# Attention and token mixer on one core: the seventh pair turned within the sixth step, the first batch's third products split over two steps

## The chip, the core and the metric

The kernel runs on one core of a Trainium2 chip. The core has a matrix engine (PE), which multiplies and transposes and writes only to PSUM, a memory of eight banks; a vector engine (DVE) and a scalar engine (ACT), which read PSUM and move results to the main on-chip memory; GpSimd (POOL), which here scales v and issues the loads; and SyncE (SP), which here issues most stores. Each engine takes its instructions in the order written and waits on semaphores for the others. The metric is the device time in microseconds (us) of one launch; lower is better. "Before" was run six times: median 99.96 us, 99.41 to 102.1.

## The reference

There are 4 batches, 8 heads, 768 tokens and 64 numbers a head. Attention without softmax and with a decay goes by blocks, with a running state of 64x64 for each head; its output is the x of a token mixer.

```python
for b in range(nb):
    intra = np.einsum('bhic,bhjc->bhij', qb, kb) * Dmask[None]
    intra = np.einsum('bhij,bhjd->bhid', intra, vb)
    inter = np.einsum('bhid,bhde->bhie', qb * lam_pow[None], kv_state)
    out[:, :, sl] = intra + inter
    kv_state = lam_block[None, :, None, None] * kv_state + np.einsum('bhsd,bhse->bhde', kb_dec, vb)
...
wq = x @ w_q
wk = x @ w_k
W_tok = scale * np.einsum('bsd,btd->bst', wq, wk)
mixed = np.einsum('bst,btd->bsd', W_tok, x)
return (np.maximum(mixed, 0.0) @ w_out).astype(np.float32)
```

`Dmask` is lower triangular with powers of lam, and `scale` is 1/8.

## The kernel before

**Pairs and steps.** Two heads of one batch are a pair; there are 16, four to a batch. The main loop (L563) makes one step a pair, n = 0 to 15. In this document "step n" and "pair n" use that count from 0, so the sixth step is step 5 and the seventh pair is pair 6. Tokens go in chunks of 128, six to a head. The decays are powers of lam put into q (`dq`) and v (`DvI`), so that the mask `maskc` is only ones and zeros.

**What a pair needs.** Three loads from POOL, `fq`, `fk` and `fv` (`load_q` L81, `load_kv` L86), 192 KB each as they land. `turn_q` (L231) transposes q with 12 PE instructions into the bank `trq`, and DVE makes qT from it, times `dq`. `turn_k` (L253) does the same into `trk`, and ACT copies it out as kT. `scale_v` (L208) makes vn, mostly on POOL. `scores` (L307) makes four banks `sc` from kT and qT, `masks` (L327) has DVE turn each into `pr`. `states` (L269) multiplies k by vn into `dps`, which holds the sums of all earlier chunks, and `sums` (L287) copies them to gs. `inter` (L334) multiplies qT by gs into two banks `oa`, `values` (L351) adds pr times vn to them, and ACT copies them to xnat, the pair's piece of x. `flip` (L375) transposes that to xT, through the bank `xp`.

**Step n** does the scores and masks of pair n, `inter` and `values` of pair n-1, the flip of pair n-2, the states and sums of pair n, and the turns of pair n+1, whose q and k must have landed by then. PE's order in it is scores, inter, values, flip, turn_q, turn_k, states.

**The mixer of a batch** runs during later steps. `mix_wk` (L396) and `mix_wq` (L416) make wkn and wqT from xT. `mix_py` (L439) multiplies wkn by xnat; ACT copies the result three times into Y. `mix_pm` (L463) makes the mixed values, 128x384 at a time, each in a bank `pm`; ACT and DVE in turn take relu and 1/8 into rmT. These are the "third products" of the change's name: eight for a batch, two for each block of 128 columns `dd`. `mix_po` (L508) multiplies rmT by the output weights `wo`, four PE instructions for 128 tokens, and ACT copies the result to osb. For batch 0 the flip of pair 3 and `mix_wk` are at the end of step 4; `mix_wq`, `mix_py`, all eight `pm` and then both turns of pair 6 are in step 5; output products of batch 0 are in steps 6 to 10 (`outs` before the turns, `late_outs` after the states).

**Order and buffers.** The order on each engine is the order of the program text; waits are put in from the data used. PSUM banks are handed out by a list: `pst` (L58) takes the bank that was free longest, `done` (L64) puts one back, and the next user of a bank waits until the engine that last read it has done so. Four banks `pm` and four `sc` are all eight.

**Loads.** All of q, k, v (but the first k), the mixer's `wqk` and `wo` are issued by POOL in program order. The start takes pairs 0 to 4; L547 to L553 issue q5, k5, `wqk`, v5 and `wo`; the dictionary `pool` (L556) gives POOL's work of steps 0 to 4 ("s4" is the scaling of v of pair 4), and later steps use `load_more` (L220). Each POOL load waits until the eighth load issued before it has landed. Stores of batch 0 wait in the list `stores` until the small transfer `late` (L579) of step 9, which waits for a late load of v.

Of the kernel before, what the change touches and what calls it, by code (L numbers as in the profile page):

```python
# [28 lines left out]
def kernel(  # L29
# [11 lines left out]
    nc = tc.nc  # L41
# [16 lines left out]
    def pst(shape, dt, name):  # L58
        i = free.pop(0)
        t = ps.tile(shape, dt, tag=f"p{i}", name=name)  # L60
        held[id(t)] = (t, i)
        return t

    def done(t):  # L64
        free.append(held.pop(id(t))[1])

    pairs = [(b, kk) for b in range(B) for kk in range(NP)]
    N = len(pairs)
# [4 lines left out]
    def q_rows(n):  # L73
        b, kk = pairs[n]
        return q[b, 2 * kk : 2 * kk + 2].rearrange("h (a p r) d -> p h a (r d)", p=128, r=2)

    def kv_rows(n, src):
        b, kk = pairs[n]
        return src[b, 2 * kk : 2 * kk + 2].rearrange("h (c p) d -> p h c d", p=128)

    def load_q(n):  # L81
        t = stage.tile([128, 2, 3, 2 * D], BF16, tag="fq", name="fq")
        nc.gpsimd.dma_start(out=t, in_=q_rows(n))  # L83
        staged[n, "q"] = t

    def load_kv(n, nm):  # L86
        t = stage.tile([128, 2, NCH, D], BF16, tag="f" + nm, name="f" + nm)
        nc.gpsimd.dma_start(out=t, in_=kv_rows(n, dict(k=k, v=v)[nm]))  # L88
        staged[n, nm] = t
# [137 lines left out]
    def turn(n):  # L227
        turn_q(n)
        turn_k(n)

    def turn_q(n):  # L231
        b, kk = pairs[n]
        fq = staged.pop((n, "q"))
        trq = pst([128, NCH, 2, 64], BF16, "trq")
        for a in range(3):
            for r in range(2):
                for hl in range(2):
                    nc.tensor.transpose(  # L238
                        trq[hl * 64 : hl * 64 + 64, 2 * a : 2 * a + 2, r, :],
                        fq[:, hl, a, r * D : (r + 1) * D],  # L240
                        ident,
                    )
        qT = tsb.tile([128, S], BF16, tag="qT", name="qT")
        nc.vector.tensor_tensor(  # L244
            out=qT,
            in0=trq.rearrange("d c r p -> d (c r p)"),
            in1=Dq[kk],
            op=ALU.mult,
        )
        done(trq)  # L250
        L[n]["qT"] = qT
# [75 lines left out]
    def masks(n, which):  # L327
        for a, hl in which:
            t = prb.tile([128, 3, CH], BF16, tag="pr", name="pr")
            nc.vector.tensor_tensor(out=t, in0=L[n]["sc"][a, hl], in1=maskc, op=ALU.mult)  # L330
            done(L[n]["sc"][a, hl])
            L[n]["pr"][a, hl] = t
# [83 lines left out]
    def mix_wq(b, kts=range(NP)):  # L416
        if 0 in kts:
            M[b]["wq"] = pst([128, HALF], F32, "wq")
        wq = M[b]["wq"]
        for kt in kts:  # L420
            for n in range(2):
                nc.tensor.matmul(  # L422
                    wq[n * 64 : n * 64 + 64, :],
                    wqk[:, 0, kt, :],
                    xT[b][:, kt, n * HALF : (n + 1) * HALF],
                    start=(kt == 0),
                    stop=(kt == NP - 1),
                    skip_group_check=True,
                )
        if NP - 1 in kts:  # L430
            wqT = hyp.tile([128, HALF], BF16, tag="wqT", name="wqT")
            nc.scalar.copy(
                out=wqT.rearrange("j (c p r) -> j c r p", c=3, r=2),
                in_=wq.rearrange("j (c r p) -> j c r p", c=3, r=2),
            )
            done(wq)
            M[b]["wqT"] = wqT
# [25 lines left out]
    def mix_pm(b, which, wide=True, engs=None):  # L463

        if isinstance(which[0], int):
            which = [(dd, n) for dd in which for n in range(2)]
        pms = [pst([128, HALF], F32, "pm") for _ in which]
        for m in range(1 if wide else 2):
            for (dd, n), pm in zip(which, pms):
                r = slice(n * 64, n * 64 + 64)  # L470
                c = (dd % 2) * CH
                if wide:
                    o, w = slice(0, 128), slice(c, c + CH)
                else:
                    o, w = slice(m * 64, m * 64 + 64), slice(c + m * 64, c + m * 64 + 64)
                nc.tensor.matmul(  # L476
                    pm[o, :],
                    M[b]["Y"][r, int(dd // 2 != n), w],
                    M[b]["wqT"][r, :],
                    start=True,  # L480
                    stop=True,
                    skip_group_check=True,
                )
        for i, ((dd, n), pm) in enumerate(zip(which, pms)):
            to = M[b]["rmT"][:, dd, n * HALF : (n + 1) * HALF]
            if engs and engs[i] is nc.vector:
                nc.vector.tensor_scalar(  # L487
                    out=to,
                    in0=pm,
                    scalar1=1.0 / 8.0,  # L490
                    scalar2=0.0,
                    op0=ALU.mult,
                    op1=ALU.max,
                )
            else:
                nc.scalar.activation(out=to, in_=pm, func=ACT.Relu, scale=1.0 / 8.0)
            done(pm)
# [10 lines left out]
    def mix_po(b, t, last=False):  # L508
# [39 lines left out]
    load_kv(5, "k")  # L548
    load_wqk()
    load_kv(5, "v")  # L550
    nc.gpsimd.dma_start(
        out=wo, in_=moe_w_out.rearrange("(kt p) (a j) -> p a kt j", p=128, j=CH)
    )  # L553


    pool = {  # L556
        0: ["q6", "s4", "k6", "v6"],
        1: ["q7", "s5", "k7", "v7"],
        2: ["q8", "k8", "s6", "v8"],
        3: ["q9", "s7", "k9", "v9"],  # L560
# [2 lines left out]
    for n in range(N):  # L563
        b, kk = pairs[n]
        for what in pool.get(n, []):
            if what[0] == "s":
                scale_v(int(what[1:]), nc.gpsimd)
            elif what[0] == "q":
                load_q(int(what[1:]))
            else:  # L570
                load_kv(int(what[1:]), what[0])
        if 11 <= n + 5 < N:
            load_more(n + 5)
        if n + 5 >= N and n + 3 < N:
            scale_v(n + 3, nc.gpsimd)
        if n == 9:

            late = consts.tile([1, D], BF16, name="late")
            nc.sync.dma_start(out=late, in_=staged[14, "v"][0:1, 0, 0, :])  # L579
            store()  # L580
        p = b - 1
        outs = {
            6: [(0, 0)],
            9: [(0, 4)],
            12: [(1, 0)],
            13: [(1, 2)],
            14: [(1, 3)],
            15: [(1, 5)],
        }.get(n, [])

        late_outs = {
            6: [(0, 1)],
            7: [(0, 2)],
            8: [(0, 3)],
            10: [(0, 5)],
            12: [(1, 1)],
            14: [(1, 4)],
        }.get(n, [])

        def back():  # L600

            if kk == 1 and n > 8:
                flip(n - 2, nc.scalar)
            if n >= 1:
                values(n - 1)
            if n >= 2 and not (kk == 1 and n > 8) and n != 5:
                flip(n - 2, nc.scalar if n < 5 else None)
            for i, t in outs:
                mix_po(i, t)
            if kk == 1 and n > 8:  # L610
                mix_wk(p)


        if n > 9 and n % 4 in (3, 0):
            mix_pm(
                (n - 5) // 4,
                [0, 1] if n % 4 == 3 else [2, 3],
                engs=(nc.scalar, nc.vector) * 2,
            )
        scores(n)  # L620
        if n >= 1:
            inter(n - 1)
        masks(n, ((0, 0), (0, 1)))
        back()

        if 1 <= n < 3:
            make_dq(n + 1)
        if n in (2, 3):
            scale_v(n, nc.vector)
        masks(n, ((1, 0),))  # L630
        if n < N - 1 and n != 5:
            turn_q(n + 1)
        masks(n, ((1, 1),))
        if n < N - 1 and n != 5:
            turn_k(n + 1)
        if n == 5:

            mix_wq(p)
            mix_py(p)
        states(n)  # L640
        if n == 4:
            flip(n - 1)
        for i, t in late_outs:
            mix_po(i, t)
        sums(n)
        if n == 0:
            scale_v(1, nc.vector)
        if n == 4:
            mix_wk(p, (0, 1, 2))
            mix_wk(p, (3,))  # L650
        if n == 5:
            for dds in ([0, 1], [2, 3]):
                mix_pm(0, dds, engs=(nc.scalar, nc.vector) * 2)
            turn(n + 1)
        if kk == 1 and n > 8:
            mix_wq(p)
            mix_py(p)
# [53 lines left out]
```

## Time and profile before

| | us |
|---|---|
| median of six runs | 99.96 |
| the profiled execution: its own time | 99.95 |
| its span, first to last instruction on the core | 98.1 |
| PE busy in the span | 85.6 |
| DVE busy | 70.9 |
| ACT busy | 62.4 |
| POOL busy | 66.8 |
| first scores of step 5 (PE) | 28.2 |
| first scores of step 6 | 34.8 |
| first scores of step 7 | 39.2 |
| first scores of step 8 | 42.8 |
| first scores of step 9 | 46.3 |
| first scores of step 10 | 51.7 |

The span's 98.1 us lie within the execution's 99.95; 1.85 us are around it. Times of single events below are counted from the span's start. Busy time is how long an engine had an instruction in work; matmuls overlap, and their ends are modelled, so a full PE isn't at its peak. A step with an output product or more of the mixer's work is longer. The loads' transfer engines are nine tenths busy or more from 2.5 to about 69 us. The clock of PE is granted in full but for one stretch at half, from 20.35 to 23.76 us.

### The profile page before, as it was taken

To read this page: it belongs to the slowest core of one execution; us is meant where nothing else is said; L and a number is where in the kernel's file an instruction comes from. 1 tells how busy PE (TensorE), PEld (TensorE's weight loads), DVE (VectorE), ACT (ScalarE), POOL (GpSimd) and SP (SyncE) were. 2 spreads that over 40 slices of the span, in tenths; PEclk is the share of its full clock that TensorE was granted. 3 is DMA by queue.
4 is the path that set the end of the run, shared out by engine and by line. 5 is a ranking of instruction groups with operands and counts; after the bars stand their busy time and mean duration, and the time that the engine had idled before them with its cause. 6 is when DMAs were issued, how large, how long until landed. Compare 5 with 4: busy or idle time off the path is not lost.

```text
span 98.1 us, 3522 instructions
## 1 busy us (share of the span) xinstructions
PE 85.6 (87%) x1507; PEld 58.0 (59%) x1507; DVE 70.9 (72%) x156; ACT 62.4 (64%) x118; POOL 66.8 (68%) x69
## 2 busy tenths in 40 slices
PE   4998677399998789999999996999999999999940
PEld 1335566387986465966788474668865466433420
DVE  6647989785976977899489999973989981273520
ACT  5085487866749945665769764667977746677230
POOL 5999999999999399999999999999060000000000
PEclk9999999966999999999999999999999999999999
DMA  0999999999999999999999999999999424325583
GB/s 7 215 148 159 166 161 162 166 164 160 168 187 157 166 168 156 145 147 134 135 153 160 133 156 132 139 141 123 272 404 395 178 107 176 145 107 213 215 313 115
DMA packets 68976, 16.79 MB, mean 171 GB/s; under 512 B 65762, under 2 KB 66018, under 8 KB 68962
## 3 DMA queue, kind: packets, MB, share of 16 engines
q0 software_dynamic: 63776, 9.90, 138.7%
q1 hardware_dynamic: 5042, 6.56, 18.4%
q8 instruction: 11, 0.18, 0.7%
q10 hardware_dynamic: 144, 0.13, 0.4%
q14 instruction: 3, 0.02, 0.1%
HBM read 20.19 MB, written 6.29 MB: 270 GB/s over the span
## 4 chain that ended last, share of the span: by engine, by line
PE 58%; DVE 15%; ACT 11%; DMA 6%; POOL 3%; issue 3%; POOLq 0%; ACTq 0%
PE po L515 19%; PE oa L359 6%; DMA fk<-in_k_dram 6%; DVE pr L330 5%; PE xp L379 5%; PE sc L317 5%; PE trq L238 5%; DVE rmT L487 4%; PE trk L258 4%; PE wq L422 3%; PE py L443 3%; PE dps L277 3%; PE wk L402 2%; ACT kT L262 2%; PE oa L341 2%
## 5 line engine op out<-in xcount | busy, mean ns | idle before, releaser
L330 DVE TENSOR_TENSOR pr<-sc,maskc 128x384 bf16<-128x384 f32 x64 | 33.3, 548 | 3.0 <-PE sc L317 2.7
L515 PE MATMUL po<-wo,rmT 128*128 128x512 bf16 (+1 forms) x100 | 23.9, 372 | 0.0
L212 POOL TENSOR_TENSOR vn<-fv,DvI 128x768 bf16<-128x768 bf16 x12 | 18.0, 1502 | 4.7 <-PE xp L379 2.8
L371 ACT CAST xnat<-oa 128x384 bf16<-128x384 f32 x31 | 13.4, 483 | 8.6 <-PE oa L359 8.5
L527 ACT COPY osb<-po 128x512 f32<-128x512 f32 (+1 forms) x22 | 12.6, 579 | 9.7 <-PE po L515 9.7
L262 ACT COPY kT<-trk 128x768 bf16<-128x768 bf16 x16 | 12.8, 801 | 7.2 <-PE trk L258 7.2
L88 POOL DMA_DIRECT2D fv<-in_v_dram x16 | 16.9, 1054 | 0.0
L88 POOL DMA_DIRECT2D fk<-in_k_dram x15 | 16.0, 1063 | 0.0
L83 POOL DMA_DIRECT2D fq<-in_q_dram x16 | 14.0, 876 | 0.8 <-POOLq L695 0.8
L515 PEld LDWEIGHTS <-rmT 128*128 128x128 bf16 x100 | 8.5, 98 | 8.5 <-issue 0.8
L317 PE MATMUL sc<-qT,kT 64*128 64x128 bf16 x192 | 8.9, 217 | 3.6 <-ACT kT L262 1.3
L244 DVE TENSOR_TENSOR qT<-trq,dq 128x768 bf16<-128x768 bf16 x16 | 8.8, 552 | 4.1 <-PE trq L238 2.9
L317 PEld LDWEIGHTS <-kT 64*128 64x128 bf16 x192 | 5.9, 94 | 8.1 <-ACT kT L262 5.6
L258 PE MATMUL trk<-ident,fk 128*64 128x128 bf16 x180 | 8.0, 226 | 2.4 <-DMA fk<-in_k_dram 2.4
L238 PE MATMUL trq<-ident,fq 128*64 128x128 bf16 x192 | 8.7, 229 | 0.0
L359 PE MATMUL oa<-vn,pr 128*128 128x64 bf16 x192 | 8.6, 196 | 0.0
L487 DVE TENSOR_SCALAR rmT<-pm 128x384 bf16<-128x384 f32 x16 | 8.0, 548 | 0.6 <-PE pm L476 0.6
L379 PE MATMUL xp<-ident,xnat 128*128 128x128 bf16 x96 | 8.3, 225 | 0.2
L277 PE MATMUL dps<-vn,fk 128*64 128x128 bf16 (+4 forms) x150 | 8.0, 239 | 0.0
L258 PEld LDWEIGHTS <-fk 128*64 128x64 bf16 x180 | 6.1, 114 | 3.1 <-DMA fk<-in_k_dram 3.1
L238 PEld LDWEIGHTS <-fq 128*64 128x64 bf16 x192 | 6.1, 113 | 3.1 <-issue 2.2
L359 PEld LDWEIGHTS <-pr 128*128 128x128 bf16 x192 | 6.8, 99 | 0.7
(62 smaller groups left out, 113.7 us busy)
## 6 DMA issues: line engine op xcount, KB each, us to landing
out_dram<-osb SPq DMA_DIRECT2D x23, 256.0 KB, 3.1
fq<-in_q_dram POOLq DMA_DIRECT2D x16, 192.0 KB, 5.7
fv<-in_v_dram POOLq DMA_DIRECT2D x16, 192.0 KB, 5.6
fk<-in_k_dram POOLq DMA_DIRECT2D x15, 192.0 KB, 6.2
wo<-in_moe_w_out_dram POOLq DMA_DIRECT2D x1, 512.0 KB, 9.4
k<-in_k_dram SPq DMA_DIRECT2D x1, 384.0 KB, 3.8
out_dram<-osb ACTq DMA_DIRECT2D x1, 128.0 KB, 2.2
out_dram<-osb SPq DMA_DIRECT2D x1, 128.0 KB, 2.1
```

The lines of the kernel that those rows point to most:

```text
L83: nc.gpsimd.dma_start(out=t, in_=q_rows(n))
L88: nc.gpsimd.dma_start(out=t, in_=kv_rows(n, dict(k=k, v=v)[nm]))
L212: eng.tensor_tensor(out=vn, in0=fv, in1=DvI[:, 2 * kk : 2 * kk + 2, :].unsqueeze(3).to_broadcast([128, 2, NCH, D]), op=ALU.mult,)
L238: nc.tensor.transpose(trq[hl * 64 : hl * 64 + 64, 2 * a : 2 * a + 2, r, :], fq[:, hl, a, r * D : (r + 1) * D], ident,)
L258: nc.tensor.transpose(trk[hl * 64 : hl * 64 + 64, c * CH : (c + 1) * CH], kn[:, hl, c, :], ident)
L262: nc.scalar.copy(out=kT, in_=trk)
L317: nc.tensor.matmul(sc[a, hl][:, cc, :], kT[r, c * CH : (c + 1) * CH], qchunk(n, r, c), start=True, stop=True, skip_group_check=True,)
L330: nc.vector.tensor_tensor(out=t, in0=L[n]["sc"][a, hl], in1=maskc, op=ALU.mult)
L359: nc.tensor.matmul(oa[hl][:, c, :], pr[c // 3, hl][:, c % 3, :], vn[:, hl, c, :], start=False, stop=(c == NCH - 1), skip_group_check=True,)
L371: nc.scalar.copy(out=to, in_=oa[hl])
L379: nc.tensor.transpose(xp[:, t, :], xnat[b][:, t, kk * CH : (kk + 1) * CH], ident)
L515: nc.tensor.matmul(po, M[b]["rmT"][:, kt, t * CH : (t + 1) * CH], wo[:, c // CH : (c + w) // CH, kt, :], start=(kt == 0), stop=(kt == 3),)
```

## The change

There are three parts, all for the work around steps 5 to 9.

- The loads q6 and k6 are issued ahead of `wo`, where they were behind it; "q6" and "k6" leave step 0's POOL list.
- In step 5 the turns of pair 6 take the places that they have in other steps: `turn_q` after the third mask, then `mix_wq`, the fourth mask, `turn_k`, and `mix_py`. Before they came last in step 5.
- Of batch 0's eight `pm`, four (blocks 0 and 1) stay at the end of step 5, and four (blocks 2 and 3) go to the head of step 7. Output products move: (0, 0) from step 6 to 7, (0, 1) from 6 to 7, (0, 2) from 7 to 8, (0, 3) from 8 to 9.

```diff
     load_kv(5, "k")
     load_wqk()
     load_kv(5, "v")
+    load_q(6)
+    load_kv(6, "k")
     nc.gpsimd.dma_start(
         out=wo, in_=moe_w_out.rearrange("(kt p) (a j) -> p a kt j", p=128, j=CH)
     )
...
     pool = {
-        0: ["q6", "s4", "k6", "v6"],
+        0: ["s4", "v6"],
         1: ["q7", "s5", "k7", "v7"],
...
         outs = {
-            6: [(0, 0)],
+            7: [(0, 0)],
             9: [(0, 4)],
...
         late_outs = {
-            6: [(0, 1)],
-            7: [(0, 2)],
-            8: [(0, 3)],
+            7: [(0, 1)],
+            8: [(0, 2)],
+            9: [(0, 3)],
             10: [(0, 5)],
...
+        if n == 7:
+            mix_pm(0, [2, 3], engs=(nc.scalar, nc.vector) * 2)
         if n > 9 and n % 4 in (3, 0):
...
         masks(n, ((1, 0),))
-        if n < N - 1 and n != 5:
+        if n < N - 1:
             turn_q(n + 1)
+        if n == 5:
+            mix_wq(p)
         masks(n, ((1, 1),))
-        if n < N - 1 and n != 5:
+        if n < N - 1:
             turn_k(n + 1)
         if n == 5:
-
-            mix_wq(p)
             mix_py(p)
         states(n)
...
         if n == 5:
-            for dds in ([0, 1], [2, 3]):
-                mix_pm(0, dds, engs=(nc.scalar, nc.vector) * 2)
-            turn(n + 1)
+            mix_pm(0, [0, 1], engs=(nc.scalar, nc.vector) * 2)
         if kk == 1 and n > 8:
```

No instruction of PE is added or taken away, and no load.

## The prediction

> **What bounds the kernel now.** [...] I read the page first, then the chain of waits in order of time, the timeline of steps 5 to 10, busy time by step, and the landing of every load.
>
> The page, for what the chain is made of:
>
> ```profile
> span 98.1 us, 3522 instructions
> PE 58%; DVE 15%; ACT 11%; DMA 6%; POOL 3%; issue 3%; POOLq 0%; ACTq 0%
> ```
>
> More than half of the chain is PE, so a change pays only where PE stands still. The chain through step 5 and the head of step 6 (start, duration, what):
>
> ```profile
> 28.25 0.44 PE sc L317 x12
> 28.69 0.14 PE oa L341 x10
> 28.83 0.46 PE oa L359 x12
> 29.29 0.77 PE wq L422 x8
> 30.06 0.67 PE py L443 x12
> 30.76 0.37 ACT Y L452
> 31.15 0.37 ACT Y L458
> 31.53 0.37 ACT Y L458
> 31.95 0.38 PE pm L476 x2
> 32.34 0.97 DVE rmT L487 x2
> 33.73 0.55 DVE rmT L487
> 34.27 0.47 DVE qT L244
> 34.79 0.51 PE sc L317 x12
> ```
>
> Here PE waits twice: for the three copies of Y before the second `pm`, and, with everything issued, for four `rmT` and then the qT of pair 6 on VectorE. Steps 6 to 9, busy time by stretch (PE, PEld, DVE, ACT, POOL, clock, DMA share, GB/s):
>
> ```profile
> 34.80:39.21 4.41, 4.41 (x83) 2.95 (x83) 3.46 (x7) 2.25 (x4) 4.21 (x5) 1.00 2.27 163
> 39.21:42.76 3.55, 3.55 (x80) 2.65 (x80) 3.09 (x7) 2.25 (x4) 3.55 (x4) 1.00 1.95 145
> 42.76:46.31 3.55, 3.55 (x80) 2.65 (x80) 3.37 (x8) 2.25 (x4) 3.55 (x5) 1.00 1.83 139
> 46.31:51.74 5.43, 5.34 (x123) 4.39 (x123) 3.54 (x10) 3.98 (x7) 5.43 (x6) 1.00 2.08 145
> ```
>
> PE is full in all four, so a product added there costs its length. Last, the load of k for pair 7 (issued at 28.62), and pair 6's k when it is turned:
>
> ```profile
> fk<-in_k_dram POOLq DMA_DIRECT2D x1, 192.0 KB, 7.8
> ```
>
> ```profile
> 33.24 0.36 PEld L258 LDWEIGHTS <-fk 128*64 128x64 bf16 x12 [0.18 <-DMA fk<-in_k_dram]
> ```
>
> Pair 7's k lands at 28.62 + 7.8 = 36.42, its q at 26.14 + 8.9 = 35.04. Step 6 now turns them at 37.39 and 37.03, with 1 to 2 us to spare.
>
> [...] Y458 x2 follow Y452 without a gap, and qT stands behind the fourth rmT. [...] The landings agree: v5 27.14, `wo` 29.85, q6 32.04, k6 33.17, v6 34.04, q7 35.04, k7 36.42, as issued. [...] The trace has one stretch at clock 0.50, 20.35 to 23.76, after a stretch in which PE was busy 1.73 of 3.41 us; a stretch with 2.50 busy was not followed by one.
>
> **The change, part by part.** Times are the profiled execution's.
>
> *Before, PE work and idle in step 5.* Chain rows and timeline: sc 0.44, inter 0.14, values 0.46, wq 0.77, py 0.67, states 0.41, eight pm at 0.107 (seven from 31.95 to 32.70) 0.86, turns 0.46 + 0.34: 4.55. From 28.25 to 34.79 are 6.54, so 1.99 idle. From there to step 10 (51.81) PE shows no wait but some 0.2 at an osb copy in step 9. The change moves PE work between steps 5 and 9 and adds none, so step 10 moves by the change in idle.
>
> *Loads.* POOL issues q6 and k6 ahead of `wo`. Each issue waits for the eighth before it to land: q6 for q4 (19.95), k6 for k4 (21.36), `wo` for v4 (22.46). So vn4 starts at about 23.9 in place of 22.65 and ends near 25.5 (1.6); step 4's states need it at 26.17, 0.65 later, else the excess falls on PE. k7 is issued at about 28.8 for 28.62. q6 lands at 27.14 + 1.1 = 28.2 (q4 and q5 took 1.0 and 1.1 after the load ahead; at worst 2.19, as now after `wo`: 29.3), k6 at 29.4 to 30.5. PE wants them at 29.29 and 30.52. `wo` lands at about 32.2, first used after 39. The bytes ahead of q7 and k7 are the same, so they land at 35.04 and 36.42; I allow 0.5 either way.
>
> *Step 5 after.* PE: values end 29.29; turn_q(6) 29.75; wq 30.52; turn_k(6) 30.86; py 31.53; states 31.94. ACT: wqT to 31.17, then kT(6) to 31.92, only then Y (1.13 for three): 33.05. First pm 32.34, three more from 33.10, step 6 scores at 33.42, in place of 34.79. Idle: 0.40 + 0.65. The stall before scores(6) goes; the Y wait grows by kT's 0.8.
>
> *Step 6 after.* It loses four pm and both output products, so the loads' cover. VectorE: rmT from 33.47 (0.37 after pm, as now), two to 34.44; two masks 35.38; xT 35.85; mask, qT, mask 37.26 (0.47 each). PE: scores to 33.86; inter waits for the bank of the second pm, rmT at 34.00 (+0.15); values and flip to 34.98; q7 with a 0.07 wake-up 35.11 (+0.13); turn_q 35.57; k7 36.49 (+0.92); turn_k, states, four pm to 37.67. kT(7) is 36.49 + 0.57 + 0.80, scores(7) at 37.91 (+0.24).
>
> *Step 7 after.* gs(6) waits for states: 37.41 to 37.89; then rmT, free at 38.42. inter(6) wants that bank: scores end 38.35, +0.11. Inter, values, flip to 39.38, first product 40.24, turns 41.04 (k8 landed at 40.0), states, second product: scores(8) at 42.42, 0.41 ahead of 42.83.
>
> *Steps 8 and 9.* Step 8 keeps one product, 3.55 (turn_k(9) at 44.26, k9 landed at 44.0). Step 9 has two: +0.97, and up to 0.12 more as wq takes 0.77 elsewhere in place of 0.65 after states. 0.97 - 0.41 = +0.56, to +0.68. ACT's copy of the moved product (0.59) falls between kT(10), done by 50.7, and wqT, which waits for wq till 51.7: nothing. SP's stores of batch 0 stand behind `late`, at 65.98, either way: nothing. The idle sum agrees: 0.40 + 0.65 + 0.15 + 0.13 + 0.92 + 0.24 + 0.11 = 2.60 against 1.99, +0.61.
>
> *On to the end.* At 53.24 the chain passes to VectorE, which has no gap until 60.57, and PE and VectorE hand over without slack after that; +0.6 goes through. The span becomes 98.7, and with the 1.85 us around it (99.95 - 98.1) the time is 100.55. The profiled 99.95 is the median 99.96 in practice, so 100.55 is compared with that.
>
> **Rivals.**
> 1. *Absorbed later.* Price 0: 99.95, not slower. VectorE has 3.54 busy of 5.43 in step 9 and 3.44 of 5.44 in the step from 64.51; if work there doesn't hang on scores(10), the delay goes into these gaps. It decides if some VectorE work of step 10 can start before 52.1. Against it: its first mask needs scores(10), and the chain is PE up to 53.22.
> 2. *Loads later.* The longer row of waits on POOL starves the queue and k7 lands 1 us later: +1.5, 101.5. For it: step 6 waits on nothing else. Against it: its 7.8 is 3.5 above the shortest landing of a load (4.3), so a backlog covers the 0.2 by which it is issued later.
> 3. *Loads earlier.* k7 by 35.4 ends that wait. VectorE is then next: masks end 37.26, gs 37.75, rmT frees the bank at 38.3, a gain of 0.15: 100.4. Only a queue shorter than 0.47 an operation would show as faster (to 99.5); three masks in 1.49 speak against it.
> 4. *The clock halves* in the step after the wait, as at 20.35: 3.41 us at half do 1.7 us of work; less 0.35 of waits, +1.35 more: 101.9. [...]
>
> **How the numbers follow.** Forecast 0.57, its own range 100.3 to 100.9 (k7 half a us early to a little late, wq). Rival 1 with half measures 0.17, rival 2 0.12, rival 3 0.07, rival 4 0.07. About 0.5% (0.5 us) can be told from no change, so slower begins at 100.46: two thirds of the forecast (0.39) and rivals 2 and 4, 0.19, with part of rival 3: 0.60. Faster: the far end of rivals 1 and 3, 0.09. Same: 0.31. The range, 99.8 to 101.6, leaves out the tail of rival 3 and rival 4.
>
> **What would show it.** Right: turns of pair 6 in the middle of step 5 without a DMA wait; scores(6) near 33.4; then PE waiting 0.8 to 1.0 on DMA for fk near 35.6 to 36.5; scores(7) near 37.9, scores(8) near 42.4, step 9 near 6.4 long. Wrong: k7 landing a us off, step 6 held elsewhere, vn4 later than 26.1, or step 10 starting at or before 51.8.

## The result, and the profile after

The changed kernel takes 100.92 us (median of 16 runs, 100.15 to 101.85) against 99.98 us (37 runs) for the kernel before. The ratio is 1.009, with a 95% interval of 1.0063 to 1.0117: between 0.6 and 1.2 us slower. The profiled execution has a span of 98.8 us. From its page, the span and what the chain is made of:

```profile
span 98.8 us, 3519 instructions
PE 44%; POOL 19%; DMA 15%; DVE 12%; ACT 3%; issue 2%; POOLq 0%
```

PE's share of the chain fell from 58% to 44%, and DMA and POOL (the loads, their issue and the scaling of v) rose from 9% to 34%. The chain of the changed kernel no longer runs through step 5; it goes back from step 7, over VectorE and the end of step 6, to the load of pair 7's k (start, duration, what):

```profile
28.71 7.35 DMA fk<-in_k_dram
...
36.10 0.53 PE trk L258 x12
36.63 0.41 PE dps L277 x10
37.04 0.28 PE pm L476 x2
37.32 0.26 DVE gs L293
37.58 0.14 issue
37.72 0.55 DVE rmT L487
38.27 0.04 issue
38.31 0.30 PE oa L341 x9
...
41.47 0.97 PE po L515 x4
42.44 0.44 PE sc L317 x12
...
50.12 0.97 PE po L515 x4
51.09 0.77 PE wq L422 x8
51.86 0.65 PE py L443 x12
52.52 0.44 PE sc L317 x12
```

Pair 7's k lands at 36.06 and is turned at once. But the chain passes over to VectorE (gs, rmT) before `inter` of step 7 can use its bank (the row `oa L341`). And step 9 has a `po` between the states and wq. Busy time of steps 6 to 9 after (columns as before):

```profile
33.40:37.58 4.18, 3.57 (x82) 2.66 (x79) 3.99 (x10) 2.43 (x6) 3.32 (x3) 1.00 2.25 165
37.58:42.38 4.80, 4.66 (x84) 3.04 (x84) 4.42 (x10) 2.97 (x6) 4.17 (x4) 1.00 1.71 126
42.38:45.93 3.55, 3.55 (x81) 2.65 (x80) 3.09 (x7) 2.24 (x4) 3.55 (x4) 1.00 1.94 146
45.93:52.46 6.53, 6.44 (x129) 4.77 (x128) 3.84 (x10) 4.58 (x8) 6.53 (x8) 1.00 2.08 144
```

In step 6 VectorE is now busy 3.99 of 4.18 us and PE only 3.57, where PE was full before. The lengths of the steps, from one first score to the next in the two timelines:

| step | before, us | after, us | difference |
|---|---|---|---|
| 5 | 6.61 | 5.57 | -1.04 |
| 6 | 4.42 | 4.18 | -0.24 |
| 7 | 3.55 | 4.80 | +1.25 |
| 8 | 3.55 | 3.55 | 0 |
| 9 | 5.43 | 6.52 | +1.09 |
| sum | 23.56 | 24.62 | +1.06 |

The gain of steps 5 and 6, 1.28, is less than what steps 7 and 9 pay, 2.34. Step 10 itself starts only 0.71 later (52.45 for 51.74), since this execution began step 5 at 27.83, 0.35 sooner. The likely reason, which no run isolates, is that it had no stretch of half clock on PE, where the profiled execution before had one from 20.35 to 23.76. A step that starts sooner and then waits for a load is longer by that much and costs nothing, so the shift of 0.71 is the better measure of this execution, and the one to hold against the forecast's 0.56 to 0.68.

One thing in step 5 is found in no view of before. From the timeline, PE's last four `py`, and further on the wait for k:

```profile
31.58 0.41 PE L443 MATMUL py<-xnat,wkn 128*64 128x256 bf16 x4 [0.76 <-issue]
...
33.59 1.02 DVE L487 TENSOR_SCALAR rmT<-pm 128x384 bf16<-128x384 f32 x2 [0.19 <-PE pm L476]
...
36.10 0.36 PEld L258 LDWEIGHTS <-fk 128*64 128x64 bf16 x12 [0.51 <-DMA fk<-in_k_dram]
...
38.55 0.52 PE L359 MATMUL oa<-vn,pr 128*128 128x64 bf16 x12
```

PE stood for 0.76 us in the middle of `py`, waiting for nothing that the profile shows. The wait for k is 0.51 (on the weight loads), not 0.92. From the first rmT (33.59) to the values of step 7 (38.55) are 4.96 us, and VectorE is busy for all of them; this interval comes back below.

### The profile page after: what moved, and what is told of

The parts are those of the page before. It is cut to its first block, busy times and chain, and to the rows that moved or that the text cites. A ratio compares the mean times of both kernels' runs of the same rounds, so it can differ in the third digit from the quotient of the medians.

```text
span 98.8 us, 3519 instructions
## 1 busy us (share of the span) xinstructions
PE 85.5 (87%) x1507; PEld 57.2 (58%) x1507; DVE 70.5 (71%) x156; ACT 62.1 (63%) x118; POOL 66.8 (68%) x69
## 4 chain that ended last, share of the span: by engine, by line
PE 44%; POOL 19%; DMA 15%; DVE 12%; ACT 3%; issue 2%; POOLq 0%
PE po L515 19%; DMA fk<-in_k_dram 15%; POOL fv L88 5%; POOL fq L83 5%; DVE pr L330 5%; POOL fk L88 4%; PE oa L359 3%; PE xp L379 3%; DVE rmT L487 3%; PE trq L238 3%; POOL vn L212 3%; PE trk L258 3%; PE dps L277 2%; PE wq L422 2%; PE wk L402 2%
## 5 line engine op out<-in xcount | busy, mean ns | idle before, releaser
L515 PE MATMUL po<-wo,rmT 128*128 128x512 bf16 (+1 forms) x100 | 23.9, 372 | 0.0
L212 POOL TENSOR_TENSOR vn<-fv,DvI 128x768 bf16<-128x768 bf16 x12 | 18.6, 1549 | 5.0 <-PE xp L379 3.0
L88 POOL DMA_DIRECT2D fv<-in_v_dram x16 | 17.5, 1091 | 0.0
L496 ACT ACTIVATE rmT<-pm 128x384 bf16<-128x384 f32 x16 | 7.1, 495 | 0.1
```

What stands on the lines that cost most here:

```text
L212: eng.tensor_tensor(out=vn, in0=fv, in1=DvI[:, 2 * kk : 2 * kk + 2, :].unsqueeze(3).to_broadcast([128, 2, NCH, D]), op=ALU.mult,)
L515: nc.tensor.matmul(po, M[b]["rmT"][:, kt, t * CH : (t + 1) * CH], wo[:, c // CH : (c + w) // CH, kt, :], start=(kt == 0), stop=(kt == 3),)
```

## The experiments

All ratios are against the kernel before, run on the same chip beside each kernel, with 95% intervals; the changed kernel has 1.009 (1.0063 to 1.0117). "My theory" in the expectations is the prediction's: the time freed in step 5 is lost in step 6, which has lost its products as cover, and step 9 pays the product that was put off.

### The parts alone

**Early loads and turns, products as before.**

```diff
-        if n == 7:
-            mix_pm(0, [2, 3], engs=(nc.scalar, nc.vector) * 2)
...
-            mix_pm(0, [0, 1], engs=(nc.scalar, nc.vector) * 2)
+            for dds in ([0, 1], [2, 3]):
+                mix_pm(0, dds, engs=(nc.scalar, nc.vector) * 2)
```

(and `outs`, `late_outs` as in the kernel before)

> The changed kernel with all eight third products of batch 0 back at the end of step 5 and its output products back in steps 6, 7 and 8; the early loads and the early turns of pair 6 stay. My theory (step 6 lost its products as cover and waits for pair 7's k and for VectorE; step 9 pays the product that was put off): with the products back, step 6 has work while the loads come, scores(7) near 39.0 for 39.27, step 9 back at 5.4 us, so 0.1 to 0.5 us faster than before, about 99.7, ratio 0.997. Rival (the early turns themselves cost, by putting kT ahead of Y on ScalarE or by moving POOL's work): still slower than before, near the changed kernel, 100.6 or more.

Measured: 99.90 us, ratio 0.9993 (0.9956 to 1.003). The loss is gone, so the turns are not what costs; the gain that I expected lies within the interval but isn't shown.

**The split alone**, on the kernel before: the other half of the diff.

> The kernel before with the third part alone: four of the third products at the head of step 7 and the output products a step later; loads and turns of pair 6 as before. My theory: scores(6) gains nothing as pair 6's k lands at 33.2, step 6 is held by VectorE, scores(8) is at or after 42.8 and step 9 pays 1.1 us, so about 1.1 us slower than before, 101.0, ratio 1.011, a little slower than the changed kernel. Rival (the turns are what costs, the split is free): the same as before, ratio within 0.003 of 1.

Measured (six runs): 101.59 us, ratio 1.017 (1.0112 to 1.0228): slower than before by more than I expected, and slower than the changed kernel, though the two intervals just meet. Its chain in steps 5 to 7:

```profile
33.27 0.04 issue
33.32 0.55 PE trk L258 x12
33.86 0.02 issue
33.89 0.81 ACT kT L262
34.69 0.05 issue
34.74 0.51 PE sc L317 x12
...
38.49 0.56 DVE rmT L487
39.05 0.04 issue
39.09 0.30 PE oa L341 x9
```

Scores(6) still start at 34.74, held by pair 6's k, which landed at 33.27. The split by itself gains nothing in step 5, and in step 7 `inter` waits for rmT until 39.09. So the split is the loss, and by the middle values the early turns win about half of it back.

**The loads alone**, on the kernel before.

```diff
     load_kv(5, "v")
+    load_q(6)
+    load_kv(6, "k")
...
-        0: ["q6", "s4", "k6", "v6"],
+        0: ["s4", "v6"],
```

> The kernel before with the first part alone: q and k of pair 6 issued ahead of the output weights, turns, third products and output products as before. My theory (the order of the loads costs nothing; scores(6) hangs on the rmT and qT on VectorE): PE's wait of 0.18 us for pair 6's k goes, scores(6) stays within 0.3 us of 34.8, the time within 0.3 us of before. Rival (the scaling of v of pair 4 and the later loads are pushed back and that is what costs): 0.5 us or more slower than before.

Measured: 100.09 us, ratio 1.0027 (1.0001 to 1.0053). In its trace steps 5 to 9 are as long as before, to 0.01 us (first scores at 27.79, 34.40, 38.82, 42.37, 45.92, 51.35), and its chain has the same rmT and qT ahead of scores(6). The trace shows no cost of the loads in these steps; the interval ends at half a per cent, so by the times alone up to about half of the loss could still be theirs.

### What holds step 6: the load, Y or VectorE?

**Y ahead of kT(6)**, on the changed kernel.

```diff
-        if n < N - 1:
+        if n < N - 1 and n != 5:
             turn_k(n + 1)
         if n == 5:
             mix_py(p)
+            turn_k(n + 1)
```

> The changed kernel with turn_k of pair 6 after the mixer's py in step 5, so that ScalarE copies Y ahead of kT(6), some 0.8 us sooner. My theory (step 6 is held by pair 7's k until 36.5, then gs and rmT on VectorE): within 0.2 us of the changed kernel, ratio against before about 1.007. Rival (the late Y is the cost, through VectorE's queue): 0.5 to 0.8 us faster than the changed kernel, ratio against before about 1.001.

Measured: 100.92 us, ratio 1.008 (1.0052 to 1.0108): no change, as expected. In the profiled execution Y was complete at 32.0 in place of 33.2. Pair 7's k landed at 36.86 there and held scores(7) to 38.38. VectorE's queue hardly began sooner, with the first rmT at 33.44 for 33.59: PE's stop made the states late, and gs, which waits for them and stands ahead of rmT, ran from 33.03. So this run doesn't show what a sooner queue would be worth. The stop was now in another instruction:

```profile
31.81 0.30 PE L258 MATMUL trk<-ident,fk 128*64 128x128 bf16 x4 [0.76 <-issue]
```

**The output weights behind pair 7's k**, on the changed kernel.

```diff
-        1: ["q7", "s5", "k7", "v7"],
+        1: ["q7", "s5", "k7", "wo", "v7"],
```

(and the load of `wo` taken from its old place)

> The changed kernel with the output weights issued after pair 7's k, so that q and k of pair 7 land some 2.5 us sooner. The wait of PE for fk in step 6 goes. My theory (VectorE's queue from the late Y on is the next lock, rmT frees the bank of inter(6) at about 38.3 either way): 0 to 0.2 us faster than the changed kernel, ratio against before about 1.007. Rival (the load alone holds step 6): scores(7) near 36.8, 0.7 to 1.0 us faster than the changed kernel, ratio against before 0.999 to 1.002.

Measured: 102.50 us, ratio 1.0241 (1.0172 to 1.031). Both theories missed, because the edit moved the wait on. k7 did land at about 33.4, but pair 8's loads now stand behind `wo`: its k landed at about 42.2 where the changed kernel had it at 40.2, and PE waited for both q8 and k8 in step 7 (1.29 and 0.79 us). Scores(7) did start at 36.80, as the rival said; the run can't tell what that would have been worth. The profiled execution was the longest of the six (104.03 us): right after that wait, from 42.2 to 45.6, its PE worked at little more than half its speed: the turn of k8 took 0.85 us, the states 1.01 and four `po` 1.89, where the same work had taken 0.50 (at 34.83), 0.60 (at 35.93) and 1.03 (at 38.58). The mean granted clock of this execution is 0.975, so this fits the prediction's rival 4, in another place. Four of the six runs have a mean clock of 0.996 or more, so the 2.4% don't come from that.

**A quarter of the output weights**, on the changed kernel, so that k7 lands sooner and no other load is put behind. Three quarters of the weights are set to zero and not loaded.

```diff
-        out=wo, in_=moe_w_out.rearrange("(kt p) (a j) -> p a kt j", p=128, j=CH)
+        out=wo[:, 0], in_=moe_w_out[:, 0:CH].rearrange("(kt p) j -> p kt j", p=128)
```

> The changed kernel with only a quarter of the output weights loaded (the first 128 of 512 output columns; the others are set to zero, so three quarters of the output are zero): 384 KB fewer stand ahead of pair 7's k, which lands about 2 us sooner, at 34 to 34.5, and no load is put behind another. PE's wait for fk in step 6 goes. My theory (from the late Y on, VectorE's queue of ten operations holds inter of step 7 at the same time): 0 to 0.3 us faster than the changed kernel, ratio against before 1.005 to 1.008. Rival (the load is what holds step 6): scores(7) and all that follows 0.7 us or more sooner, ratio against before 1.001 or less.

Measured: 100.52 us, ratio 1.0036 (1.0012 to 1.0059): less of a gain than the rival's, and by the middle value more than mine. Pair 7's k landed at about 33.9, 2.2 us sooner, and the wait for it is gone. From the timeline (its lines are one further down than in the changed kernel):

```profile
33.07 1.02 DVE L488 TENSOR_SCALAR rmT<-pm 128x384 bf16<-128x384 f32 x2 [0.76 <-PE pm L477]
...
35.06 0.50 PE L259 MATMUL trk<-ident,fk 128*64 128x128 bf16 x12
...
36.52 0.23 PE L318 MATMUL sc<-qT,kT 64*128 64x128 bf16 x1
...
38.03 0.52 PE L360 MATMUL oa<-vn,pr 128*128 128x64 bf16 x12
```

Scores(7) start 1.06 us sooner than in the changed kernel (37.58), the values of that step only 0.52 sooner (38.55). From the first rmT to those values it is 38.03 - 33.07 = 4.96 us, the same as with the late k, and again VectorE is busy throughout. So in these two executions VectorE's queue sets this interval, and the load is hidden in it. The 0.52 us are the sooner start of the queue: here PE didn't stop in `py`. This run lacks the late load and the stop together; the product in step 11, below, shows the late load without the stop.

### The stop of PE in step 5

**Four warming matmuls fewer**, on the changed kernel (`WARM` 5 to 3, `WARM2` 4 to 2).

> The changed kernel with four warming matmuls (eight PE instructions) fewer at the start. The changed kernel's PE stops for 0.76 us behind the eighth product py of step 5, with nothing that the profile shows to wait for; in two other versions it stops at the same count of PE instructions, once within the turns. If PE runs out of instructions there, the stop moves by four products, to the end of py; if it belongs to py or its data, it stays behind the eighth. The time is within 0.5 us of the changed kernel either way.

Measured once, 101.91 us; one run says nothing of half a us. The stop moved:

```profile
32.05 0.60 PE L277 MATMUL dps<-vn,fk 128*64 128x320 bf16 x10 [0.55 <-issue]
```

All twelve `py` now run through, and PE stops behind them, eight instructions later in the work and so at the same count. The stop belongs to a count of PE's instructions and not to `py`.

### What the put-off product costs

**Product (0, 3) in step 11 in place of step 9**, on the changed kernel.

```diff
-            9: [(0, 3)],
             10: [(0, 5)],
+            11: [(0, 3)],
```

> The changed kernel with the output product (0, 3) in step 11 in place of step 9. My theory: the 1.1 us that step 9 grew by is this product on a full PE, while steps 11 and 12 are bound by VectorE and PE stands idle there for 0.3 to 0.6 us a step; so step 9 is 5.4 us again, step 11 grows by 0.2 to 0.6, and the time falls by 0.5 to 0.9 us against the changed kernel, to about the time of before, ratio 0.999 to 1.004. Rival (step 9 is slow for another reason, such as the late rows of Y): no change from the changed kernel, ratio 1.008.

Measured: 99.90 us, ratio 0.9989 (0.9963 to 1.0016): the whole loss is gone with this one move. Step 9 is 5.43 us again; in its chain wq follows the states directly:

```profile
50.35 0.26 PE dps L277 x10
50.60 0.65 PE wq L422 x8
51.26 0.65 PE py L443 x12
51.91 0.44 PE sc L317 x12
```

From the first scores of step 10 to those of step 13 are 12.78 us, for 12.77 before, so step 11 takes the product at no cost.

Up to step 8 this is the changed kernel, so the trace is a second one of its steps 5 to 8. PE didn't stop in it, and step 5, which began at 28.58, took 4.79 us. But pair 7's k landed at 36.70, and it held step 6:

```profile
36.74 0.53 PE L258 MATMUL trk<-ident,fk 128*64 128x128 bf16 x12 [0.75 <-DMA fk<-in_k_dram]
...
37.79 0.49 DVE L293 CAST gs<-dps 128x320 bf16<-128x320 f32 x1 [0.41 <-PE dps L277]
```

VectorE stood for 0.41 us before gs, and from the first rmT (33.57) to the values of step 7 (39.03) are 5.46 us in place of 4.96. Step 9 began at 46.41, later than the 45.93 of the execution with the stop.

**The same product from step 8 to step 11**, on the kernel before, and on the version with the early turns (next section).

> The kernel before with the output product (0, 3) moved from step 8 to step 11 and nothing else. My theory: as before less 0.6 to 0.9 us, about 99.3, ratio 0.991 to 0.994, as step 8 gets shorter by a product and step 11 hides most of it. Rival (step 11 pays it in full): ratio 1.000.

Measured: 99.84 us, ratio 0.9996 (0.9975 to 1.0017): nothing, so my theory was wrong here. Its chain at the end of step 8:

```profile
45.31 0.22 DVE qT L244
45.53 0.16 issue
45.69 0.55 DVE pr L330
46.23 0.41 DVE gs L293
46.64 0.04 issue
46.69 0.32 PE oa L341 x10
```

With a product less, step 8 is held by VectorE's masks and gs. A full PE doesn't mean that a product's length can be saved: in step 8 of the kernel before VectorE was next, busy for 3.37 of 3.55 us. In step 9 it was busy only 3.54 of 5.43 us, and there the product costs its length (0.97 of the 1.09 us by which that step grew).

### Versions that were to beat both

**Early turns, all eight third products in step 5, and Y ahead of kT(6)** (the edits of the first and the fourth experiment together).

> The early loads and turns with all eight third products at the end of step 5 and the output products as before (as in the first experiment), and turn_k of pair 6 after the mixer's py, so that ScalarE copies Y ahead of kT(6). With the products as cover step 6 waits for no load, so here an earlier Y should pay, where in the changed kernel it did not: 0.3 to 0.5 us faster than the first experiment, about 99.5, ratio against before 0.993 to 0.997. Rival (step 6 is bound by loads in this version too, or by VectorE's four rmT, whatever Y does): the same as the first experiment, ratio 0.999.

Measured: 99.70 us, ratio 0.9976 (0.9946 to 1.0006). In its one trace steps 5 to 9 take 23.26 us, for 23.56 before and 23.83 in the first experiment. The times show neither gain: the interval holds 1, and that of the first experiment (0.9993) overlaps it.

**The same with product (0, 3) in step 11.**

> The early loads and turns, all eight third products in step 5, turn_k(6) behind py, output products as before but for (0, 3), which goes from step 8 to step 11. My theory (a product on a full PE costs 1 us in step 8, and 0.1 to 0.3 us in step 11, where VectorE is the bound): 0.7 us or so faster than the version without that move, about 99.0, ratio against before 0.988 to 0.993. Rival (the loads of k for pairs 11 and 12, paced by POOL, hold the steps from 10 on): the same as without the move, ratio 0.997.

Measured: 99.90 us, ratio 0.9986 (0.9952 to 1.002): no gain, for the reason seen in step 8 above.

**And with the copies of xT in steps 5 to 8 on ScalarE**, so that VectorE has less to do.

```diff
-                flip(n - 2, nc.scalar if n < 5 else None)
+                flip(n - 2, nc.scalar if n < 9 else None)
```

> The version with the early loads and turns, all eight third products in step 5, turn_k(6) behind py and the product (0, 3) in step 11, with the copies of xT in steps 5 to 8 on ScalarE in place of VectorE. My theory, as the last two experiments changed it: taking the product out of step 8 gave nothing because VectorE, with 3.4 to 3.5 us of work a step, holds step 8 as soon as PE has less; with 0.47 us less on VectorE a step, step 8 is 0.4 to 0.5 us shorter, up to where pair 9's k lands (44.0), so 0.3 to 0.6 us faster than that version, ratio against before 0.993 to 0.996. Rival (pair 9's k holds step 8, whatever VectorE does): no change, ratio 0.998.

Measured: 99.92 us, ratio 0.9991 (0.9966 to 1.0017). Neither theory named the cause:

```profile
43.31 0.86 ACT xnat L371 x2
44.17 0.71 ACT xT L385
44.88 0.10 issue
44.98 0.81 ACT kT L262
45.78 0.05 issue
45.83 0.51 PE sc L317 x12
```

Now ScalarE is late: the copy of xT stands ahead of kT(9), and the scores wait for it. In this step of 3.49 us PE is busy for 2.64, VectorE for 2.91 and ScalarE for 2.95, and taking work from one shows the next. None of these versions is shown to beat the kernel before.

## Why the prediction was right, and where it was not

1. *Direction.* Slower, at 100.55, was forecast; 100.92 was measured, inside the stated range and a hair above the forecast's own one (100.3 to 100.9). The forecast's +0.6 lies at the low edge of what was measured, 0.6 to 1.2.
2. *Step 5: the mis-sized term.* Scores(6) were put at 33.42, 5.17 us after scores(5); they came at 33.40, but 5.57 after. That the times agree is luck, for two errors met: the step began 0.35 sooner, and PE then stopped for 0.76, where the sum had nothing for PE's own instruction stream. In the run with a quarter of the weights, without a stop, scores(6) came 4.78 after scores(5) (28.09 to 32.87), so the rest of the sum was some 0.4 too long. What the stop adds to the whole time stays open: with it and k at 36.06 step 9 began at 45.93, without it and k at 36.70 at 46.41.
3. *Step 6: the right two holders, in the other order.* The prediction put 0.92 us of PE's idle time down to pair 7's k, and named VectorE as the next lock, 0.15 us behind (its rival 3). Measured: k landed at 36.06, 0.36 sooner than taken, PE waited 0.51, and the bank came free at 38.27, against the 38.3 of that rival. The unchanged 4.96 us with a k 2.2 us sooner shows that VectorE's queue was the later lock in this execution. Where k lands at 36.70 or 36.86, as in the executions with the product in step 11 and with Y ahead of kT(6), the load takes over: VectorE waits for the states behind it, 0.41 and 0.72.
4. *Step 7.* Scores(8) were forecast at 42.42; the chain has 42.44. Step 9 began at 45.93, 0.38 sooner than before, for the forecast's 0.41. In the two executions with a later k it began at 46.41 and 46.58, later than the 46.31 before. So the gain in steps 5 to 8 seems to hang on when the loads land, which may be why the middle of many runs lies above the forecast; three traces don't show that.
5. *Steps 8 and 9.* 3.55 and +0.97 to +1.09 were forecast, 3.55 and +1.09 measured, the wq at 0.77 included. The move of this product to step 11 took the whole loss away, so this is the term that decides.
6. *Costs put at nothing.* Pair 6 was turned in the middle of step 5 without a wait for its loads: q6 and k6 were issued at 20.53 and 21.75, 0.49 and 0.30 after the eighth load before each had landed, and landed at 28.13 and 29.35. v of pair 4 was scaled from 23.96 to 25.79, for the 23.9 to 25.5 forecast, in time for states that began at 25.85; the margin was 0.06 and not 0.65, since the scaling took 1.83 for 1.6 and the step came sooner. With the fewer warming matmuls and the same loads PE did wait for it, 0.32. The change of order of the loads by itself is worth 0 to 0.5%.
7. *Rivals.* Nothing absorbed the delay by itself (rival 1): step 11 has room, but the product was put in step 9. Loads a whole us later and the halved clock did not occur in the profiled execution; the mean clock was 0.991 or more in every run of the changed kernel, where the profiled execution before, with its 3.41 us at half, has 0.983.

## What to carry to other kernels

Work that seems to be in the way of a stalled stage can be the cover of the next: before it is moved, add up for that next stage what each other engine has to do, and take the longest. Price a move at both ends: here a product put into a stage cost its length where VectorE and ScalarE had slack (step 9, 3.54 and 3.98 of 5.43 us busy, +1.09 us), and taken out of one saved nothing where a second engine was nearly as full (step 8, ratio 0.9996). Put it where the chain runs through another engine, as in step 11 here (12.78 us for three steps, for 12.77).

## What the runs showed of the hardware

PE stopped where the profile shows nothing that it waited for. In the traces of nine versions with the early turns six show a stop at the same count of PE instructions: for 0.76 us in the changed kernel, 0.68 in the first experiment, 0.76 with Y ahead of kT(6), 0.55 with the fewer warming matmuls, and 0.41 and 0.34 in the first two of the versions that were to beat both. The transfers include a queue of kind "instruction", with 12 transfers of some 16 KB in the changed kernel (0.20 MB in all). In the two stretches below, 28.9 to 29.5 us of the changed kernel and 28.3 to 28.9 of the run with a quarter of the weights, there is one such transfer each (packets, MB, share of 16 engines):

```profile
q8 instruction: 1, 0.02, 9.9%
```

```profile
q8 instruction: 1, 0.02, 9.3%
```

In the first it ran from 29.27 to 30.22 (9.9% of 16 engines in 0.6 us are 0.95 us on one), and PE went on at 31.58, 1.36 us after its end. In the second it ran from 28.45 to 29.34, and PE, which came to that count at 30.91, 1.57 us after its end, didn't stop. In the kernel before it ran from 29.14 to 30.03, and PE came to that count at about 32.8, having waited for Y, 2.75 us after its end, and didn't stop either. That PE had run out of instructions and waited for this transfer fits these three times, but it is a reading: no run took the transfer away by itself, and none shows what sets its time. Step 5 of the changed kernel, which was made to come sooner, met the stop.
